# Keeping late loads and state work behind the MLP tiles in a fused memory attention and MLP kernel

## The chip, the cores and the metric

The kernel runs on one core of a Trainium2 chip. The metric is the device time of one execution in microseconds, lower is better. Besides plain times there is one profiled execution, which the hardware profiler recorded instruction by instruction. The engines in that profile are PE (TensorE matmul, with PEld for its weight loads), DVE (VectorE), ACT (ScalarE), POOL (GpSimd) and SP (SyncE, which here only issues DMA transfers). SPq and ACTq are the DMA issues of SP and ACT.

## The reference

Eight batches hold eight heads of 512 tokens with 64 numbers each (x), and each head has a state of 32 vectors. Tokens read from the state and the state reads from the tokens. Both results of a batch, 544 rows of 512 numbers, go through an MLP with a squared ReLU.

```python
scores  = scale * x @ state.T           # softmax over the 32 vectors -> a
xread   = a @ state
scores2 = scale * state @ x.T           # softmax over the 512 tokens -> a2
sread   = a2 @ x
rows    = concat([xread, sread], axis=2) -> (8 * 544, 512)
out     = relu(rows @ w_in) ** 2 @ w_out      # w_in 512 x 2048, w_out 2048 x 512
```

w_in and w_out come as doubles. They are read as pairs of 32-bit words and turned into singles on the chip.

## The kernel before, in words

For the token rows the kernel never forms xread. Since xread = a @ state for each head, xread @ w_in = a @ z with z = state @ w_in, where z has 256 rows for a batch (eight heads of 32 vectors), in two groups of 128. z is made once for each half of the batches: batches 0 to 3 early (`z_part` with G = 0), batches 4 to 7 later. It is written to DRAM tiles (`zd`) and fetched for each batch and each 256 columns (`z_fetch`, tile `z_raw`).

**Precision.** Most operands are split in two (`split`, lines 96 to 98): ACT casts a high part, another engine subtracts it to get the low part. A product is then three matmuls. The first two batches' scores and the first six pieces of z are computed in plain fp32 instead (`PLAIN_X`, `PLAIN_Z`).

**The MLP tile.** The main loop goes through 144 MLP tiles. A tile takes 128 of the 2048 hidden columns for 512 rows: `up` makes six matmuls (L392, tile `ph`), then ReLU on ACT (L394), the square on ACT for the first ten tiles and on DVE (L398) after them, and a split into `g_hi` and `g_lo`. `down`, two tiles later, makes twelve matmuls (L418) into the four sums `po0` to `po3`. Counting tiles from 0, the order is batch 0 (tiles 0 to 5), batch 1 (6 to 15), batch 0 again (16 to 25), batch 1 again (26 to 31), batch 2 from tile 32, batch 3 from tile 48 and so on to tile 127. The last 16 tiles are the 256 state rows. When a batch's part ends, DVE and ACT copy or add the four `po` into the batch's result (L437, L439; L599 where a first part is there already).

**What surrounds the tiles.** Each column block of w_in is loaded (L156, `w_raw`, 512 KB), turned into singles (`singles`: L108 on ACT, then L109, L113, L117 on DVE, tile `wf`), written back to DRAM for later (L162), and multiplied with the state into z (L191 plain, L203 split). Each row block of w_out is loaded (`wo_load`, L444), converted by the same lines (tile `wof`) and split (`wo_hi`, `wo_lo`). For each batch, `pad` loads and splits the state (`sp_raw`, `sp_hl`), `load_t` and `load_n` load x in two layouts (`xt_raw`, `xn_raw`, 512 KB each, two groups a batch), `cut_t` and `cut_n` split them, `scores` makes the scores (`pst`, or `pq` and `st`), `soft1` and `soft1b` make the softmax for the tokens, ending with a transpose into `at` (L327) and the split into `a_hi`, `a_lo`. `turn` scales the exponentials of the second softmax (L338 to L340) and transposes them on PE, `read` makes sread.

**What sets the order.** The program text calls these steps between the MLP tiles: `Ahead` spreads them evenly up to a due tile (two slots a tile). That order is not binding. A scheduler that builds the program with its own timing model may issue an instruction earlier on its engine's queue, if its inputs and buffers are there. Every engine, and SP's DMA issues, then run their queue strictly in order. An instruction that waits holds up all behind it on its engine. `tc.issue_after(i)` adds a constraint for the scheduler: what is traced inside the block and runs on the engine of i is queued behind i. It is a rule of order, with no wait at run time.

Raw loads of weights share four buffers (tag `raw`), x loads two (`xraw`). The scores' PSUM tiles and those of z share two banks (`px`), and `ph` has two.

Of the kernel before, what the change touches and what calls it, by code (L numbers as in the profile page):

```python
# [9 lines left out]
F32 = mybir.dt.float32  # L10
# [8 lines left out]
def memory_attention_then_relu2_ffn(  # L19
# [22 lines left out]
    nc = tc.nc  # L42
# [3 lines left out]
    H = C // D  # L46
# [47 lines left out]
            zd[G, k] = dr.tile([P, NG, HG, FW], F32, name=f"zd_{G}_{k}")  # L94

    def split(hi, lo, src, eng_lo):
        nc.scalar.copy(out=hi, in_=src)  # L97
        eng_lo.tensor_sub(out=lo, in0=src, in1=hi.bitcast(F32))  # L98

    def singles(out_f, words):  # L100

        low, high = words[..., 0], words[..., 1]
        bits = out_f.bitcast(I32)
        nc.scalar.activation(out_f, high.bitcast(F32), AF.Abs, scale=2.0**-112)  # L108
        nc.vector.tensor_scalar(  # L109
            out=bits, in0=bits, scalar1=3, scalar2=0x7FFFFFF8,  # L110
            op0=ALU.logical_shift_left, op1=ALU.bitwise_and,
        )
        nc.vector.scalar_tensor_tensor(  # L113
            out=bits, in0=high, scalar=-0x80000000, in1=bits,
            op0=ALU.bitwise_and, op1=ALU.bitwise_or,
        )
        nc.vector.scalar_tensor_tensor(  # L117
            out=bits, in0=low, scalar=29, in1=bits,
            op0=ALU.logical_shift_right, op1=ALU.bitwise_or,
        )  # L120


    def z_state(G):
        if G == 0:
            raw = sb.tile([P, H, GB * N], F32, name="st_f", tag="x_hl", bufs=1)
            st["raw"] = raw
        else:
            raw = sb.tile([P, H, GB * N], F32, name="st_raw", tag="raw", bufs=RAW)
        for j in range(2):
            nc.sync.dma_start(out=raw[j * D:(j + 1) * D].rearrange("d h m -> d (h m)"), in_=stT[G])  # L130
        hi = sb.tile([P, H, GB * N], F32R, name="stz_hi", bufs=1)
        lo = sb.tile([P, H, GB * N], F32R, name="stz_lo", bufs=1)
        if G:
            split(hi, lo, raw, nc.gpsimd)
        else:
            for i in range(2):
                own = slice(i * D, (i + 1) * D)
                other = slice((1 - i) * D, (2 - i) * D)
                for v in (hi, lo):
                    nc.gpsimd.memset(v[other, i::2, :].bitcast(F32), 0.0)  # L140
                split(hi[own, i::2, :], lo[own, i::2, :], raw[own, i::2, :], nc.vector)
        st[G] = hi, lo

    def z_part(G, k, g):
# [5 lines left out]
        def load():  # L150
            if G:
                box["wf"] = sb.tile([P, nq, FW], F32, name="wf", bufs=2)
                nc.sync.dma_start(out=box["wf"], in_=wd[k][:, ccs, :])
                return
            raw = sb.tile([P, nq, FW, 2], I32, name="w_raw", tag="raw", bufs=RAW)
            nc.sync.dma_start(out=raw.rearrange("p c f w -> p (c f w)"), in_=w_in[k * NG + g])  # L156
            box["raw"] = raw

        def convert():
            wf = sb.tile([P, nq, FW], F32, name="wf", bufs=2)  # L160
            singles(wf, box["raw"])
            nc.sync.dma_start(out=wd[k][:, ccs, :], in_=wf)  # L162
            box["wf"] = wf

# [216 lines left out]
    def mlp(width, fcs, first, rows, aux):  # L381

        nt = width // P
        po = []
        gs = {}
        last = len(fcs) - 1

        def up(fc):
            ph = ps_h.tile([P, S], F32, name="ph", tag="ph")[:, :width]
            todo = first(fc)  # L390
            for i, (w, v) in enumerate(todo):
                nc.tensor.matmul(ph, lhsT=w, rhs=v, start=i == 0, stop=i == len(todo) - 1)  # L392
            r = sb.tile([P, S], F32, name="r", bufs=2)[:, :width]
            nc.scalar.activation(r, ph, AF.Relu)  # L394
            if units[0] < 10:
                nc.scalar.activation(ph, r, AF.Square)
            else:
                nc.vector.tensor_mul(out=ph, in0=ph, in1=r)  # L398
            units[0] += 1
            hi = sb.tile([P, S], F32R, name="g_hi", bufs=2)[:, :width]  # L400
            lo = sb.tile([P, S], F32R, name="g_lo", bufs=2)[:, :width]
            split(hi, lo, ph, nc.vector)
            gs[fc] = hi, lo

        def down(i):
            fc = fcs[i]
            hi, lo = gs.pop(fc)
            if not po:
                po.extend(
                    ps_o.tile([P, DM], F32, name=f"po{t}", tag="po") for t in range(nt)  # L410
                )
            todo = [(t, j) for t in range(nt) for j in range(3)]
            if i < last:
                todo.sort(key=lambda tj: tj[1] == 2)
            for t, j in todo:
                g = (hi, hi, lo)[j][:, t * P:(t + 1) * P]
                w = wo[fc // FPC][j % 2][:, fc % FPC, :]
                nc.tensor.matmul(  # L418
                    po[t], lhsT=g, rhs=w, start=i == 0 and j == 0, stop=i == last and j == 2
                )  # L420
# [257 lines left out]
```

## Time and profile before

| what | value |
|---|---|
| time, median of 3 runs | 707.23 us (707.12 to 707.27) |
| profiled execution, its own time | 708.43 us |
| span of the profiled execution | 706.6 us |
| PE busy | 669.8 us (95%) |
| DVE, ACT, POOL busy | 452.2, 398.3, 199.3 us |
| bytes moved by DMA | 90.58 MB |
| mean clock granted to TensorE | 0.973 |

The profile gives start and duration of each instruction, what its engine waited for, and the granted TensorE clock. Matmuls are pipelined: one of 512 columns is shown as some 400 ns long, while the next one starts much sooner. The reading has to go by stage, since the first hundred microseconds and the rest have different limits. The time of the profiled execution is 1.8 us above its span, and 1.2 us above the median of the plain runs.

### The profile page before, as it was taken

The numbers are of one execution on the slowest core, as the hardware profiler recorded it, in microseconds if no ns is written. First come the engines' busy times: TensorE is split into PE (matmuls) and PEld (weight loads), VectorE is DVE, ScalarE is ACT, GpSimd is POOL, SyncE is SP. The second block draws the span as 40 slices with busy tenths as digits, with TensorE's granted clock in tenths as the row PEclk, the third lists the DMA queues.
The fourth block names the chain that finished last, engine by engine and source line by source line (L and its number), as shares of the span: only waits on it lengthen the run. The fifth ranks groups of instructions, "written<-read, shape, count | busy, mean of one in ns | idle before, by whom it ended". The sixth has DMA issues, their size and how long they took to land.

```text
span 706.6 us, 9753 instructions
## 1 busy us (share of the span) xinstructions
PE 669.8 (95%) x3152; PEld 551.6 (78%) x3152; DVE 452.2 (64%) x757; ACT 398.3 (56%) x727; POOL 199.3 (28%) x181
## 2 busy tenths in 40 slices
PE   4688789999999999999999999999999999999997
PEld 2355668778888888888888878888888888888996
DVE  4859999758456944447945794797944445443553
ACT  3767687567565863467735653665654344332442
POOL 2314433345443540053403240344242022000000
PEclk8589999999999999999999999999999999999999
DMA  8898899435363542344423312412241112100421
GB/s 276 270 315 283 258 306 315 131 97 153 98 202 122 166 149 62 102 135 120 135 78 120 87 48 74 139 58 90 89 150 61 30 31 90 31 16 0 130 80 32
DMA packets 74548, 90.58 MB, mean 128 GB/s; under 512 B 7680, under 2 KB 57600, under 8 KB 74496
## 3 DMA queue, kind: packets, MB, share of 16 engines
q1 hardware_dynamic: 56896, 72.90, 32.9%
q10 hardware_dynamic: 17600, 17.04, 7.1%
q8 instruction: 25, 0.41, 0.3%
q14 instruction: 27, 0.22, 0.1%
HBM read 60.03 MB, written 29.88 MB: 127 GB/s over the span
## 4 chain that ended last, share of the span: by engine, by line
PE 79%; DVE 8%; DMA 6%; issue 2%; ACT 2%; SPq 1%; POOL 0%; DVEq 0%; ACTq 0%; POOLq 0%
PE po L418 47%; PE ph L392 25%; PE pz L203 3%; DMA wo_raw<-w_out 2%; PE pr L355 2%; DMA sp_raw<-stP 2%; PE pq L288 1%; PE pt L343 1%; DVE wf L117 1%; DVE wf L113 1%; DVE z_lo L98 1%; DVE g_lo L98 1%; DMA zd<-z_stage 1%; DMA xt_raw<-xT 1%; DVE wf L109 1%
## 5 line engine op out<-in xcount | busy, mean ns | idle before, releaser
L418 PE MATMUL po<-wo_hi,g_hi 128*128 128x512 f32 x544 | 217.3, 400 | 0.6 <-ACT g_hi L97 0.5
L418 PE MATMUL po<-wo_lo,g_hi 128*128 128x512 f32 x544 | 215.0, 395 | 0.0
L398 DVE TENSOR_TENSOR ph<-ph,r 128x512 f32<-128x512 f32 (+1 forms) x134 | 89.1, 665 | 169.1 <-ACT r L394 168.9
L394 ACT ACTIVATE r<-ph 128x512 f32<-128x512 f32 (+1 forms) x144 | 82.1, 572 | 171.0 <-PE ph L392 169.6
L418 PE MATMUL po<-wo_hi,g_lo 128*128 128x512 f32 x544 | 152.2, 392 | 0.0
L418 PEld LDWEIGHTS po<-wo_hi,g_hi 128*128 128x128 f32 x544 | 103.9, 191 | 22.4 <-ACT g_hi L97 2.0
L418 PEld LDWEIGHTS po<-wo_lo,g_hi 128*128 128x128 f32 x544 | 103.9, 191 | 19.5
L418 PEld LDWEIGHTS po<-wo_hi,g_lo 128*128 128x128 f32 x544 | 101.5, 189 | 21.1 <-issue 1.0
L98 DVE TENSOR_TENSOR g_lo<-ph,g_hi 128x512 fp32r<-128x512 f32 (+1 forms) x144 | 94.4, 656 | 36.3 <-ACT g_hi L97 27.7
L97 ACT CAST g_hi<-ph 128x512 fp32r<-128x512 f32 (+1 forms) x144 | 81.0, 563 | 57.9 <-DVE ph L398 51.7
L392 PE MATMUL ph<-a_hi,z_hi 128*128 128x512 f32 x256 | 81.4, 399 | 2.6 <-DVE nm L306 1.5
L392 PE MATMUL ph<-a_lo,z_hi 128*128 128x512 f32 x256 | 80.1, 392 | 0.0
L392 PE MATMUL ph<-a_hi,z_lo 128*128 128x512 f32 x256 | 80.0, 394 | 0.0
L98 POOL TENSOR_TENSOR xn_hl<-xn_raw,xn_hl 128x1024 fp32r<-128x1024 f32 x16 | 38.9, 2432 | 138.0 <-ACT xn_hl L97 71.2
L182 POOL TENSOR_TENSOR w<-wf,w 64x512 fp32r<-64x512 f32 x32 | 43.0, 1343 | 74.9 <-ACT w L181 69.8
L392 PEld LDWEIGHTS ph<-a_hi,z_hi 128*128 128x128 f32 x256 | 47.6, 190 | 15.2 <-DVE g_lo L98 2.1
L392 PEld LDWEIGHTS ph<-a_hi,z_lo 128*128 128x128 f32 x256 | 48.5, 190 | 10.4
L392 PEld LDWEIGHTS ph<-a_lo,z_hi 128*128 128x128 f32 x256 | 48.2, 189 | 10.5 <-issue 0.3
L98 POOL TENSOR_TENSOR xt_hl<-xt_raw,xt_hl 128x1024 fp32r<-128x1024 f32 x12 | 28.9, 2406 | 75.4 <-ACT xt_hl L97 43.7
L98 DVE TENSOR_TENSOR z_lo<-z_raw,z_hi 128x512 fp32r<-128x512 f32 x64 | 47.9, 750 | 0.3 <-DMA wd<-wf 0.3
L97 ACT CAST z_hi<-z_raw 128x512 fp32r<-128x512 f32 x64 | 39.2, 615 | 1.3 <-DMA wd<-wf 0.8
L98 POOL TENSOR_TENSOR wo_lo<-wof,wo_hi 128x512 fp32r<-128x512 f32 x16 | 25.2, 1578 | 51.4 <-ACT wo_hi L97 51.4
(97 smaller groups left out, 833.7 us busy)
## 6 DMA issues: line engine op xcount, KB each, us to landing
zd<-z_stage ACTq DMA_DIRECT2D x64, 256.0 KB, 3.2
z_raw<-zd SPq DMA_DIRECT2D x252, 64.0 KB, 2.4
xt_raw<-xT SPq DMA_DIRECT2D x16, 512.0 KB, 3.8
w_raw<-w_in SPq DMA_DIRECT2D x16, 512.0 KB, 5.3
wo_raw<-w_out SPq DMA_DIRECT2D x16, 512.0 KB, 5.8
xn_raw<-xn SPq DMA_DIRECT2D x16, 512.0 KB, 3.9
out<-sum SPq DMA_DIRECT2D x32, 256.0 KB, 2.5
wd<-wf SPq DMA_DIRECT2D x16, 256.0 KB, 3.7
```

Of the source, the lines that this page charges most:

```text
L97: nc.scalar.copy(out=hi, in_=src)
L98: eng_lo.tensor_sub(out=lo, in0=src, in1=hi.bitcast(F32))
L109: nc.vector.tensor_scalar(out=bits, in0=bits, scalar1=3, scalar2=0x7FFFFFF8, op0=ALU.logical_shift_left, op1=ALU.bitwise_and,)
L113: nc.vector.scalar_tensor_tensor(out=bits, in0=high, scalar=-0x80000000, in1=bits, op0=ALU.bitwise_and, op1=ALU.bitwise_or,)
L117: nc.vector.scalar_tensor_tensor(out=bits, in0=low, scalar=29, in1=bits, op0=ALU.logical_shift_right, op1=ALU.bitwise_or,)
L182: nc.gpsimd.tensor_sub(out=w[other], in0=wf[own], in1=w[own].bitcast(F32))
L203: nc.tensor.matmul(pz[:, q, :], lhsT=a[:, h, :], rhs=w, start=j == 0, stop=j == len(todo) - 1,)
L355: nc.tensor.matmul(pr[:, q].rearrange("p i c -> p (i c)"), lhsT=my["e"][:, t, q].rearrange("p i n -> p (i n)"), rhs=my["xn"][:, t, q].rear ...
L392: nc.tensor.matmul(ph, lhsT=w, rhs=v, start=i == 0, stop=i == len(todo) - 1)
L394: nc.scalar.activation(r, ph, AF.Relu)
L398: nc.vector.tensor_mul(out=ph, in0=ph, in1=r)
L418: nc.tensor.matmul(po[t], lhsT=g, rhs=w, start=i == 0 and j == 0, stop=i == last and j == 2)
```

## The change

The change does three things.

1. It keeps some steps back. `marks` remembers, for each engine, the latest weight load on SP (L156, L444) and the latest split of an MLP tile on ACT and DVE, as traced so far. The steps in `late` are traced behind these marks: `pad` of batches 2 to 7, every `turn`, and `load_t` and `load_n` of batches 1 to 7. Their instructions on SP, ACT and DVE then cannot be queued ahead of the mark.
2. The state for z of the first four batches (`st_f`) is loaded with only the heads that each half of the rows uses: 4 of 8 heads, 128 KB instead of 256 KB for each half, in pieces of 512 bytes instead of 4096.
3. The split of that state (`z_state_cut`) is traced after the conversions of the first four w_in blocks and the first z products, and on DVE behind the last conversion step of the second block.

No arithmetic is added or removed.

```diff
+    def behind_marks():
+        stack = ExitStack()
+        for i in marks.values():
+            stack.enter_context(tc.issue_after(i))
+        return stack
...
         for j in range(2):
-            nc.sync.dma_start(out=raw[j * D:(j + 1) * D].rearrange("d h m -> d (h m)"), in_=stT[G])
+
+            heads = slice(None) if G else slice(j, None, 2)
+            nc.sync.dma_start(out=raw[j * D:(j + 1) * D, heads, :], in_=stT[G, :, heads, :])
...
-            nc.sync.dma_start(out=raw.rearrange("p c f w -> p (c f w)"), in_=w_in[k * NG + g])
+            mark(nc.sync.dma_start(out=raw.rearrange("p c f w -> p (c f w)"), in_=w_in[k * NG + g]))
...
-            split(hi, lo, ph, nc.vector)
+            mark(*split(hi, lo, ph, nc.vector))
...
-        nc.sync.dma_start(
+        mark(nc.sync.dma_start(
             out=raw.rearrange("p e w -> p (e w)"), in_=w_out[fc * P:(fc + 1) * P, :]
-        )
+        ))
...
     def emit(step):
-        step()
+        with behind_marks() if step in late else ExitStack():
+            step()
...
+    late = {attentions[b][1] for b in range(PLAIN_X, B)}
+    late |= {w["turn"] for b in range(B) for w in attentions[b][2]}
+    late |= {w[n] for b in range(1, B) for w in attentions[b][2] for n in ("load_t", "load_n")}
...
-        q["cut_t"], q["scores"], q["soft1"], p["soft1b"], q["soft1b"], lambda: z_state(0),
+        q["cut_t"], q["scores"], q["soft1"], p["soft1b"], q["soft1b"], lambda: z_state_load(0),
         z0[0][1], z0[0][2], z0[1][1], z0[1][2], *z0[0][3], *z0[1][3], z0[2][0], z0[3][0],
     ):
         emit(s_)
+
+    with tc.issue_after(z0[1][4]["done"].ins):
+        z_state_cut(0)
```

Adding lines moves line numbers: L162 before is L186 after, L156 is L180, L444 is L468, L245 is L269, L264 is L288, L340 is L364, L599 is L631, L327 is L351, L392 is L416, L418 is L442.

Three places of the built order matter later. The first is the queue of SP at the start of the program. Before:

```order
L130 DMA st_f<-stT 64x1024 x2
L156 DMA w_raw<-w_in 128x1024 x2
L245 DMA sp_raw<-stP 128x128 x2
L264 DMA xt_raw<-xT 128x2x512 x2
L162 DMA wd_83<-wf 128x512
L156 DMA w_raw<-w_in 128x1024
L245 DMA sp_raw<-stP 128x128 x2
L162 DMA wd_83<-wf 128x512
L444 DMA wo_raw<-w_out 128x1024
```

With the change:

```order
L150 DMA st_f<-stT 64x4x128 x2
L180 DMA w_raw<-w_in 128x1024 x2
L269 DMA sp_raw<-stP 128x128
L186 DMA wd_83<-wf 128x512
L180 DMA w_raw<-w_in 128x1024
L186 DMA wd_83<-wf 128x512
L468 DMA wo_raw<-w_out 128x1024
```

The states of batches 2 to 4 and both x loads of batch 1 have left this place. The x loads of batch 1 now stand behind the third and the fifth w_out load, those of batch 2 behind the last w_out load.

The second place is the start of DVE's queue, where the second w_in block is converted (`wf_188` before, `wf_178` now). Before:

```order
L338 TENSOR_SCALAR s2_130<-s2_130 128x1
L322 TENSOR_REDUCE s1_151<-q1_124 128x16
L315 TENSOR_REDUCE m1_147<-q1_139 128x16
L306 TENSOR_SCALAR nm2_141<-nm2_141 128x1
L98 TENSOR_TENSOR sp_hl_77<-sp_raw_1688,sp_hl_77 64x4x32 x2
L117 SCALAR_TENSOR_TENSOR wf_188<-w_raw_119,wf_188 128x512
L339 RECIPROCAL s2_130<-s2_130 128x1
L323 TENSOR_SCALAR s1_151<-s1_151 128x16
L338 TENSOR_SCALAR s2_145<-s2_145 128x1
L340 TENSOR_SCALAR e2_129<-e2_129,s2_130 128x512
```

With the change:

```order
L339 TENSOR_REDUCE m1_147<-q1_139 128x16
L346 TENSOR_REDUCE s1_151<-q1_124 128x16
L330 TENSOR_SCALAR nm2_141<-nm2_141 128x1
L131 SCALAR_TENSOR_TENSOR wf_178<-w_raw_119,wf_178 128x512
L98 TENSOR_TENSOR stz_lo_222<-st_f_169,stz_hi_221 64x4x128 x2
L347 TENSOR_SCALAR s1_151<-s1_151 128x16
L123 TENSOR_SCALAR wf_249<-wf_249 128x512
```

The split of batch 2's state (`sp_hl`) and the scaling of the second softmax of batch 0 (`s2`, `e2`) are gone from here, and the split of the state for z (`stz_lo`) moved behind the conversion. The scaling of batch 1, too, no longer stands among the first tiles.

The third place is DVE's queue where batch 2 begins (tile 32). `at_1896` is the second head group of batch 2's softmax, from which `a_hi` comes; `ph_1877` is tile 31, `ph_1944` tile 32; `sum_1238` is batch 1's result. Before, `at_1896` stood at tile 22:

```order
L338 TENSOR_SCALAR s2_1827<-s2_1827 128x1
L339 RECIPROCAL s2_1827<-s2_1827 128x1
L340 TENSOR_SCALAR e2_1826<-e2_1826,s2_1827 128x512
L98 TENSOR_TENSOR g_lo_1474<-ph_1463,g_hi_1473 128x512
L322 TENSOR_REDUCE s1_1891<-q1_1821 128x16
L398 TENSOR_TENSOR ph_1509<-ph_1509,r_1525 128x512
L323 TENSOR_SCALAR s1_1891<-s1_1891 128x16
L98 TENSOR_TENSOR e_hl_2035<-pt_2030,e_hl_2035 128x8x64
L324 RECIPROCAL s1_1891<-s1_1891 128x16
L98 TENSOR_TENSOR g_lo_1529<-ph_1509,g_hi_1528 128x512
L327 STREAM_TRANSPOSE at_1896<-q1_1821 128x512
```

With the change it stands at the end of tile 31:

```order
L98 TENSOR_TENSOR g_lo_1888<-ph_1877,g_hi_1887 128x512
L346 TENSOR_REDUCE s1_1891<-q1_1821 128x16
L347 TENSOR_SCALAR s1_1891<-s1_1891 128x16
L348 RECIPROCAL s1_1891<-s1_1891 128x16
L631 TENSOR_TENSOR sum_1238<-sum_1238,po0_1759 128x512
L631 TENSOR_TENSOR sum_1238<-sum_1238,po1_1760 128x512
L631 TENSOR_TENSOR sum_1238<-sum_1238,po2_1761 128x512
L631 TENSOR_TENSOR sum_1238<-sum_1238,po3_1762 128x512
L351 STREAM_TRANSPOSE at_1896<-q1_1821 128x512
L422 TENSOR_TENSOR ph_1944<-ph_1944,r_1960 128x512
```

The four adds that need the finished sums of tile 31 now stand ahead of the transpose that tile 32 needs. On PE, the place is this, with the change:

```order
L442 MATMUL po3_1762<-wo_hi7_1383,g_lo_1888 128x512
L416 MATMUL ph_1989<-a_hi_1686,z_hi_1950 128x512
L416 MATMUL ph_1944<-a_hi_1686,z_hi_1950 128x512
L416 MATMUL ph_1944<-a_hi_1686,z_lo_1951 128x512 x2
L416 MATMUL ph_1944<-a_lo_1687,z_hi_1950 128x512
```

The first row is the last product of tile 31, and `ph_1989` is tile 33. The third row is the first that reads the second head group of `a_hi`.

More of the change, by code (lines that the diff above doesn't have):

```diff
@@ L96, in split, with mark @@
     def split(hi, lo, src, eng_lo):
-        nc.scalar.copy(out=hi, in_=src)
-        eng_lo.tensor_sub(out=lo, in0=src, in1=hi.bitcast(F32))
+        a = nc.scalar.copy(out=hi, in_=src)
+        return a, eng_lo.tensor_sub(out=lo, in0=src, in1=hi.bitcast(F32))
+    marks = {}
+    def mark(*those):
+        for i in those:
+            marks[i.ins.engine] = i.ins
+    def behind_marks():
[3 more added lines that the diff above has]
+        return stack
     def singles(out_f, words):
@@ L116, in singles @@
         )
-        nc.vector.scalar_tensor_tensor(
+        return nc.vector.scalar_tensor_tensor(
             out=bits, in0=low, scalar=29, in1=bits,
@@ L123, in z_state, with z_state_load @@
     def z_state(G):
+        z_state_load(G)
+        z_state_cut(G)
+    def z_state_load(G):
         if G == 0:
@@ L129, in z_state, with z_state_cut @@
         for j in range(2):
-            nc.sync.dma_start(out=raw[j * D:(j + 1) * D].rearrange("d h m -> d (h m)"), in_=stT[G])
+            heads = slice(None) if G else slice(j, None, 2)
+            nc.sync.dma_start(out=raw[j * D:(j + 1) * D, heads, :], in_=stT[G, :, heads, :])
+        st["raw", G] = raw
+    def z_state_cut(G):
+        raw = st["raw", G]
         hi = sb.tile([P, H, GB * N], F32R, name="stz_hi", bufs=1)
@@ L160, in convert @@
             wf = sb.tile([P, nq, FW], F32, name="wf", bufs=2)
-            singles(wf, box["raw"])
+            box["done"] = singles(wf, box["raw"])
             nc.sync.dma_start(out=wd[k][:, ccs, :], in_=wf)
@@ L218, in product @@
             return run
-        return load, convert, cut, [product(i) for i in range(2)]
+        return load, convert, cut, [product(i) for i in range(2)], box
     def z_fetch(b, k):
@@ L503, in memory_attention_then_relu2_ffn @@
     zs = [[z_part(G, k, g) for k in range(NFCH) for g in range(NG)] for G in range(NGB)]
+    late = {attentions[b][1] for b in range(PLAIN_X, B)}
+    late |= {w["turn"] for b in range(B) for w in attentions[b][2]}
+    late |= {w[n] for b in range(1, B) for w in attentions[b][2] for n in ("load_t", "load_n")}
     lags = {}
-    for _, _, c, ps in zs[0] + zs[1]:
+    for _, _, c, ps, _ in zs[0] + zs[1]:
         lags[ps[0]] = [(c, 2)]
@@ L657 @@
             state.reshape(B * N // 128, 128 // N, H, N, D).transpose(0, 4, 2, 1, 3)
-        ).reshape(B * N // 128, D, H * 128),
+        ),
         "stP": np.ascontiguousarray(
```

## The prediction, made before the result was known

> **What bounds the kernel now.** I read the page first, then the busy time by stage, then PE's waits.
>
> ```profile
> span 706.6 us, 9753 instructions
> PE   4688789999999999999999999999999999999997
> DVE  4859999758456944447945794797944445443553
> ```
>
> PE is full from the seventh of the 40 slices on. Only the start has room. By stage (columns: stretch, its length, busy us of PE, PEld, DVE, ACT and POOL with instruction counts, granted TensorE clock, DMA share, GB/s):
>
> ```profile
> 0.00:28.50 28.50, 12.34 (x32) 6.06 (x32) 16.45 (x36) 15.68 (x34) 9.44 (x17) 0.73 0.86 276
> 28.50:43.00 14.50, 11.09 (x33) 6.85 (x33) 11.41 (x19) 10.44 (x21) 4.75 (x4) 0.74 0.89 293
> 43.00:53.00 10.00, 10.00 (x30) 6.96 (x31) 5.55 (x11) 4.44 (x9) 1.28 (x1) 0.78 0.88 311
> 53.00:70.00 17.00, 14.55 (x59) 10.59 (x58) 15.32 (x27) 13.25 (x25) 7.68 (x5) 0.90 0.84 279
> 70.00:100.00 30.00, 22.40 (x110) 18.46 (x111) 29.93 (x49) 22.47 (x44) 11.17 (x7) 0.92 0.88 283
> 100.00:130.00 30.00, 30.00 (x143) 25.30 (x142) 29.42 (x43) 20.88 (x38) 10.71 (x7) 0.97 0.88 281
> 130.00:160.00 30.00, 28.68 (x132) 23.47 (x131) 17.64 (x29) 20.42 (x36) 12.26 (x8) 1.00 0.34 99
> 160.00:240.00 80.00, 79.72 (x387) 66.88 (x386) 55.13 (x96) 51.63 (x95) 36.68 (x30) 1.00 0.48 149
> 240.00:655.00 415.00, 414.50 (x1947) 345.44 (x1946) 247.26 (x407) 218.18 (x384) 105.28 (x103) 1.00 0.27 83
> ```
>
> PE is idle 16.2 us before 28.5, 3.4 in the next stretch, 2.5 in 53 to 70 and 7.6 in 70 to 100: 29.6 us. From 100 to 655 it is idle 2.1 us. From 70 to 130 DVE is full (29.93 and 29.42 of 30) and DMA busy at 0.88. So the start is bound by weights that arrive and are converted, its second part by DVE; after it every microsecond that PE waits is lost. PE's waits (us in total, times, longest):
>
> ```profile
> PE pz L191 <- DVE wf L117: 11.7, 4, 4.0
> PE pst L298 <- DMA xt_raw<-xT: 4.9, 1, 4.9
> PE pz L203 <- ACT w L97: 2.5, 2, 2.2
> PE ph L392 <- DVE nm L306: 1.5, 1, 1.5
> ```
>
> The largest is for converted w_in blocks; the fourth is the one long stall after 100 us, in the stretch 130 to 160.
>
> **The change at the start.** By the built order these DVE instructions leave the part ahead of tile 6: the split of batch 2's state and the four scalings of the second softmax of batches 0 and 1, with eight one-column steps. Their rows, and two others that matter (start, us, what):
>
> ```profile
> 18.79 1.33 DVE L98 TENSOR_TENSOR sp_hl<-sp_raw,sp_hl 64x128 fp32r<-64x128 f32 x2
> 21.43 0.48 DVE L340 TENSOR_SCALAR e<-e,s 128x512 f32<-128x512 f32 x1
> 22.34 1.27 DVE L340 TENSOR_SCALAR e<-e,s 128x512 f32<-128x512 f32 x1
> 60.96 0.14 DVE L338 TENSOR_SCALAR s<-s 128x1 f32<-128x1 f32 x1
> 62.87 0.47 DVE L340 TENSOR_SCALAR e<-e,s 128x512 f32<-128x512 f32 x1
> 65.32 2.47 DVE L98 TENSOR_TENSOR w<-wf,w 128x512 fp32r<-128x512 f32 x1 [1.61 <-ACT w L97]
> 77.34 0.41 DVE L109 TENSOR_SCALAR wof<-wof 128x512 int32<-128x512 int32 x1
> 78.86 0.68 DVE L117 SCALAR_TENSOR_TENSOR wof<-wo_raw,wof 128x512 int32<-128x512 int32 x1
> 80.13 0.68 DVE L98 TENSOR_TENSOR w<-wf,w 128x512 fp32r<-128x512 f32 x1
> 81.41 1.51 DVE L340 TENSOR_SCALAR e<-e,s 128x512 f32<-128x512 f32 x1
> ```
>
> The split is 1.33, the scalings 0.48 + 1.27 + 0.47 + 1.51 = 3.73, the small steps 8 times 0.15 = 1.2: 6.3 us. One split of a weight took 2.47 instead of 0.68 while POOL split batch 2's x; that work leaves too, so 1.8 more. Against that, the order pulls one w_out conversion (0.41 + 0.68 + 0.68) and one weight split (0.68) ahead of tile 6: 2.45. Net 6.3 + 1.8 - 2.45 = 5.6 us of DVE work less.
>
> What of this is gain? Where DVE is full, 70 to 100, and PE idle, a DVE microsecond is a PE microsecond. Before 70 DVE itself is idle 12.05 + 3.09 + 4.45 + 1.68 = 21 us, waiting for w_in, so work removed there may only lengthen that idle time. Lower bound of the gain 0: all falls there. Upper bound: all PE idle time of 53 to 100 disappears, 2.45 + 7.60 = 10. I take 4.5, nearer to 5.6 than to either end, since the stretched split and the 1.51 scaling (3.3 us net) lie where DVE is the bound. A gain of 0 to 0.9 us from the shorter state load (256 KB less at 276 GB/s), ahead of which PE waits 4.9 us for x, is inside this.
>
> The transfers taken from the start, by the order three x loads of 512 KB (two of batch 2, one of batch 0's second layout), three states of 64 KB and 256 KB of z's state, are 1984 KB, or 7.2 us at 283 GB/s. They free the queue for w_in and w_out, which shortens the same waits; I do not add it to the DVE gain. The x loads of batch 1, moved behind the third and fifth w_out load, are read only after tile 5; with a landing some 6 us from issue I cost them at nothing. If they came late, tile 6 would wait.
>
> The waits of 130 to 160 (1.32) and 160 to 655 (0.78) are shuffled by the new order: between 0 and -2.1, taken -1.0.
>
> **The change at tile 32.** Batch 2's softmax, done by tile 22 before, now comes at tiles 29 to 31, and the order puts four `sum` adds of tile 31 ahead of the transpose into `at`. The rows (first the chain of waits: start, us on PE; then DVE's timeline; then groups: busy us, mean ns | idle before them):
>
> ```profile
> 185.46 4.53 PE po L418 x20
> 163.57 1.40 DVE L294 TENSOR_TENSOR st<-pq,st_low 64x512 f32<-64x512 f32 x2 [0.36 <-ACT st_low L293]
> 176.88 0.71 DVE L327 STREAM_TRANSPOSE at<-q 128x512 f32<-128x512 f32 x1 [1.29 <-POOL q L325]
> L599 DVE TENSOR_TENSOR sum<-sum,po 128x512 f32<-128x512 f32 x8 | 5.2, 679 | 0.0
> L327 DVE STREAM_TRANSPOSE at<-q 128x512 f32<-128x512 f32 x16 | 11.3, 706 | 2.8 <-POOL q L325 2.5
> L97 ACT CAST a_hi<-at 128x512 fp32r<-128x512 f32 x16 | 9.8, 620 | 10.4 <-DVE at L327 8.4 <-PE ph L392 1.9
> L394 ACT ACTIVATE r<-ph 128x512 f32<-128x512 f32 x128 | 75.9, 595 | 145.4 <-PE ph L392 144.0 <-DMA z_raw<-zd 0.6 <-ACT z_stage L215 0.4
> L398 DVE TENSOR_TENSOR ph<-ph,r 128x512 f32<-128x512 f32 x118 | 82.2, 696 | 146.9 <-ACT r L394 146.6
> L97 ACT CAST g_hi<-ph 128x512 fp32r<-128x512 f32 x128 | 75.0, 587 | 56.9 <-DVE ph L398 50.7 <-PE po L418 2.7 <-PE ph L392 2.3
> ```
>
> A product takes 4.53 / 20 = 0.2265 us. The first add waits for `po0`, finished four products before the last, so at T0 (PE's last product of tile 31) less some 0.7 the adds begin. Four times 0.679 brings them to T0 + 2.0, `at` to 2.7, `a_hi` to 3.35. PE has one product behind T0, 0.23: it waits **3.1**. Without the adds, the softmax chain itself, 163.57 to 177.59 = 14.0 us in the old place, stands against some 47 products and 8 half ones, 11.6 us, that PE has from the scores to T0: a wait of the same size, so dropping the adds' share would not save it all. Lower bound 0: the adds or the softmax run ahead of this estimate, as far as `po` allows.
>
> Then the ten products left of tiles 32 and 33 run 2.3 us, to T0 + 5.6. Tile 32's `down` needs r 0.595, square 0.696, g_hi 0.587, one z cast in between on ACT at 0.6; 2.5 us less what overlaps the second tile's products. `ph` has two buffers, so no later `up` can start. PE waits again, **2.3**. What follows is slow matmuls: the next rows show a wait of 2.18 and one of 1.08 and PE after it.
>
> ```profile
> 97.50 0.39 PE L203 MATMUL pz<-w,stz_lo 128*128 128x256 f32 x1 [2.18 <-ACT w L97]
> 99.09 0.58 PE L203 MATMUL pz<-w,stz_hi 128*128 128x256 f32 x1 [1.08 <-DVE w L98]
> 101.39 0.63 PE L418 MATMUL po<-wo_hi,g_hi 128*128 128x512 f32 x1
> 101.81 0.47 PE L418 MATMUL po<-wo_lo,g_hi 128*128 128x512 f32 x1
> ```
>
> Starts 0.42 apart instead of 0.23, from 99.1 to 101.8: half rate, 2.7 us in which 1.35 are lost. I take 1.5 for tile 32, bounds 0 and 2.5. [...]
>
> Sum at tile 32: 3.1 + 2.3 + 1.5 = 6.9; I take 6.5, since the first wait of 3.1 assumes that every piece runs at its mean. Bounds 2.5 (the refill of the pipeline alone, if `a_hi` is in time but tile 32's `up` not ahead) and 9 (a softmax 2 us later).
>
> **Sum.** -4.5 - 1.0 + 6.5 = +1.0. The profiled execution's own time is 708.43, so 709.4 in its terms. It lies 1.2 above the median of 707.23, so the forecast is **708.2 us**.
>
> **Rivals.** B, the start gives everything. 70 to 100 is full of DVE work and the transfers free 7.2 us as well; if all 10 us of PE's idle time there go and tile 32 costs 5: 707.23 - 10 + 5 = 702.2. For it: DVE's 29.93 of 30. Against: PE waits longest for w_in blocks (11.7 us), all of it before 43 us, where DVE has room.
>
> C, slower: the start gives nothing. The pacing chain there is load, cast, three DVE steps and product of each w_in block, whose loads are in the order as before; the removed 6.3 us lay in DVE's idle 21 us and the pulled-ahead conversion eats the rest. Tile 32 stays at 6.5 and the old stalls give 0.5: 707.23 + 6.5 - 0.5 = 713. It decides when the start gains under 4 us, and is clear at 0. For it: DVE idle before 70. Against: 3.3 us of relief after 65 us, where DVE is full.
>
> D, the stall at tile 32 stays small (2.5 or less), since the scheduler put the adds first but the sums of `po` come earlier than I place them: 707.23 - 4.5 - 1 + 2.5 = 704.2. Against: `po3` cannot be finished before T0, and its add stands ahead of `at`.
>
> E, as the forecast, but PE's clock stays full at tile 32: 708.2 - 1.5 = 706.7, no change. For it: the stall of 1.5 in 130 to 160 left the granted clock at 1.00. Against: the rows of 97 to 102 us.
>
> That the change does not do what it says is excluded by the rows of the order.
>
> **How the numbers follow.** Forecast .35, E .15, B .24, C .20, D .06. A measurement of this kernel tells about 0.2% from no change, 1.4 us, so 705.8 to 708.6 is no change. The forecast and E together spread over 705 to 711.5, by the 0 to 10 of the start's gain around its middle; of their .50 I put .10 faster, .21 the same, .19 slower. B (.24) and D (.06, less .01) are faster, C (.20) slower. That is .39, .22 and .39. The range takes in B's 702.2 with a microsecond below it and ends at C's 713: 701 to 713.
>
> **What would show it.** Start: DVE in the stretch 70 to 100 no longer full, PE's waits for `w` and `wf` shorter by 3 to 6 us, the first twelve tiles earlier by as much. B: no idle time of PE between 53 and 100. C: tile 6 at the same time as before. Tile 32: a wait of PE in `ph`, named after `a_hi`, of 2.5 to 3.5 us, with four L631 rows on DVE just ahead of the L351 row; a second of some 2 us in `po` named after `g_hi`; then matmuls 0.42 us apart for 2 to 3 us, and the granted clock of that stretch under 1. E: spacing of 0.23 right after. D: no wait there over 1.5 us. The forecast falls as a whole if any other batch's first tile (48, 64, 80, 96, 112, 128) shows a wait over 1 us, which I have costed at nothing, since their softmax stands tiles ahead in the new order, or if the x of batch 1 comes too late for tile 6.

## The result, and the profile of the changed kernel

The change made the kernel slower: median 716.2 us (715.58 to 717.36) beside 707.25 us before, a ratio of 1.0126 with a 95% interval of 1.0108 to 1.0143. The same kernel on another chip later gave 713.2 beside 707.16, ratio 1.0088 (1.0062 to 1.0115). So it costs 6 to 9 us. The forecast was 708.2 in a range of 701 to 713; both results lie above it.

The changed kernel's profiled execution took 716.28 us, 7.85 more than the one before. Its page, and its busy time by stage from 70 us on (columns as in the prediction; the first 130 us follow further down as one row):

```profile
span 714.1 us, 9749 instructions
...
PE 672.7 (94%) x3152; PEld 554.3 (78%) x3152; DVE 457.6 (64%) x757; ACT 399.0 (56%) x727; POOL 199.5 (28%) x181
```

```profile
70.00:100.00 30.00, 21.94 (x111) 19.13 (x110) 29.97 (x45) 22.34 (x43) 11.67 (x7) 0.89 0.89 283
...
130.00:160.00 30.00, 30.00 (x137) 24.92 (x136) 14.27 (x21) 16.58 (x29) 8.02 (x5) 1.00 0.36 112
160.00:240.00 80.00, 75.01 (x328) 61.10 (x327) 45.35 (x80) 37.89 (x71) 18.32 (x13) 0.96 0.26 84
```

and from there to 655 us:

```profile
240.00:655.00 415.00, 412.87 (x1959) 345.58 (x1958) 263.08 (x440) 234.55 (x412) 129.02 (x123) 1.00 0.30 95
```

From these rows and those of before, PE's idle time by stage:

| stage, us | PE idle before | PE idle after | what the prediction said of it |
|---|---|---|---|
| 0 to 130 | 29.6 | 29.2 | start, -4.5 |
| 130 to 160 | 1.3 | 0.0 | old stalls, -1.0 with the next ones |
| 160 to 240 | 0.3 | 5.0 | tile 32, +6.5 with the slow clock |
| 240 to 655 | 0.5 | 2.1 | nothing |

Idle time explains 4.6 us of the span's 7.5 (over the whole span, 36.8 before and 41.4 after). The rest is PE's longer busy time (672.7 against 669.8). In the stretch 160 to 240 the granted clock was 0.96 instead of 1.00: it stood at 0.50 for two steps of 3.41 us, from 216.32 and from 223.15 on (their rows are in the last section). PE worked through both and lost half of each, 3.4 us. Counted in the same way, by the trace's clock, PE lost 13.8 us up to 130 us before and 14.7 after, so the start did not gain there either.

The new loss stands where the prediction put it, at tile 32. PE's waits there, then DVE's queue:

```profile
215.88 0.50 PE L416 MATMUL ph<-a_hi,z_hi 128*128 128x512 f32 x1 [2.94 <-ACT a_hi L97]
...
221.89 0.50 PE L442 MATMUL po<-wo_hi,g_hi 128*128 128x512 f32 x1 [1.88 <-ACT g_hi L97]
...
223.58 0.63 PE L442 MATMUL po<-wo_hi,g_hi 128*128 128x512 f32 x1
224.01 0.63 PE L442 MATMUL po<-wo_lo,g_hi 128*128 128x512 f32 x1
...
303.90 0.50 PE L442 MATMUL po<-wo_hi,g_hi 128*128 128x512 f32 x1 [1.20 <-ACT g_hi L97]
```

```profile
212.07 2.48 DVE L631 TENSOR_TENSOR sum<-sum,po 128x512 f32<-128x512 f32 x4 [0.56 <-PE po L442]
214.47 0.70 DVE L351 STREAM_TRANSPOSE at<-q 128x512 f32<-128x512 f32 x1
```

The four adds run first, from 212.07, then the transpose; PE goes on 0.7 us after the transpose ends, once `a_hi` is cast, and has waited 2.94 us. The refill of the pipeline costs 1.88. At 223.58 products start 0.43 us apart; the undisturbed spacing was 0.2265. The last PE row, at tile 48, is a wait that the prediction had costed at nothing.

### The profile page after: what moved, and what is told of

Read it like the earlier page. It is cut to its first block, busy times and chain, and to the rows that moved or that the text cites. A ratio compares the mean times of both kernels' runs of the same rounds, so it can differ in the third digit from the quotient of the medians.

```text
span 714.1 us, 9749 instructions
## 1 busy us (share of the span) xinstructions
PE 672.7 (94%) x3152; PEld 554.3 (78%) x3152; DVE 457.6 (64%) x757; ACT 399.0 (56%) x727; POOL 199.5 (28%) x181
## 4 chain that ended last, share of the span: by engine, by line
PE 80%; DMA 7%; DVE 6%; ACT 3%; issue 2%; SPq 1%; ACTq 0%; DVEq 0%
PE po L442 47%; PE ph L416 25%; PE pr L379 2%; PE pz L227 2%; DMA zd<-z_stage 2%; DMA w_raw<-w_in 2%; PE pq L312 2%; DMA wo_raw<-w_out 1%; DVE wof L127 1%; PE pt L367 1%; DMA sp_raw<-stP 1%; DVE wf L127 1%; DVE wf L131 1%; SPq L254 1%; DMA z_raw<-zd 1%
## 5 line engine op out<-in xcount | busy, mean ns | idle before, releaser
L442 PE MATMUL po<-wo_hi,g_hi 128*128 128x512 f32 x544 | 215.8, 397 | 5.2 <-ACT g_hi L97 5.1
L442 PE MATMUL po<-wo_lo,g_hi 128*128 128x512 f32 x544 | 214.4, 394 | 0.0
L418 ACT ACTIVATE r<-ph 128x512 f32<-128x512 f32 (+1 forms) x144 | 82.5, 574 | 158.4 <-PE ph L416 156.1
L442 PE MATMUL po<-wo_hi,g_lo 128*128 128x512 f32 x544 | 152.3, 391 | 0.2 <-DVE g_lo L98 0.2
L442 PEld LDWEIGHTS po<-wo_hi,g_hi 128*128 128x128 f32 x544 | 103.5, 190 | 28.7 <-ACT g_hi L97 7.2
L98 DVE TENSOR_TENSOR g_lo<-ph,g_hi 128x512 fp32r<-128x512 f32 (+1 forms) x144 | 94.4, 656 | 42.1 <-ACT g_hi L97 30.1
L442 PEld LDWEIGHTS po<-wo_lo,g_hi 128*128 128x128 f32 x544 | 103.4, 190 | 20.7 <-issue 0.2
L442 PEld LDWEIGHTS po<-wo_hi,g_lo 128*128 128x128 f32 x544 | 100.8, 188 | 20.4 <-DVE g_lo L98 0.4
L416 PE MATMUL ph<-a_hi,z_hi 128*128 128x512 f32 x256 | 82.0, 400 | 5.3 <-ACT a_hi L97 4.4
L416 PE MATMUL ph<-a_lo,z_hi 128*128 128x512 f32 x256 | 81.7, 396 | 0.0
L416 PE MATMUL ph<-a_hi,z_lo 128*128 128x512 f32 x256 | 81.5, 399 | 0.0
L98 POOL TENSOR_TENSOR xn_hl<-xn_raw,xn_hl 128x1024 fp32r<-128x1024 f32 x16 | 38.5, 2408 | 150.3 <-ACT xn_hl L97 127.0
L416 PEld LDWEIGHTS ph<-a_hi,z_hi 128*128 128x128 f32 x256 | 48.0, 192 | 16.5 <-ACT a_hi L97 5.5
L416 PEld LDWEIGHTS ph<-a_lo,z_hi 128*128 128x128 f32 x256 | 49.1, 192 | 11.2 <-issue 0.7
L416 PEld LDWEIGHTS ph<-a_hi,z_lo 128*128 128x128 f32 x256 | 49.0, 192 | 10.3
L98 POOL TENSOR_TENSOR xt_hl<-xt_raw,xt_hl 128x1024 fp32r<-128x1024 f32 x12 | 28.9, 2405 | 94.4 <-ACT xt_hl L97 71.4
L98 DVE TENSOR_TENSOR z_lo<-z_raw,z_hi 128x512 fp32r<-128x512 f32 x64 | 49.2, 768 | 0.1
L239 ACT COPY z_stage<-pz 128x512 f32<-128x512 f32 x64 | 37.5, 590 | 10.3 <-PE pz L227 5.7
```

Source lines behind the costliest of these rows:

```text
L98: return a, eng_lo.tensor_sub(out=lo, in0=src, in1=hi.bitcast(F32))
L239: nc.scalar.copy(out=stage, in_=pz)
L442: nc.tensor.matmul(po[t], lhsT=g, rhs=w, start=i == 0 and j == 0, stop=i == last and j == 2)
```

## The experiments

Each run's time stands beside runs of the kernel before on the same chip.

| run | median us | ratio to before, 95% interval |
|---|---|---|
| late_only | 718.5 | 1.0151 (1.0129 to 1.0174) |
| state_only | 707.07 | 0.9986 (0.9972 to 1.0000) |
| b2_free | 704.08 | 0.9957 (0.9939 to 0.9976) |
| no_wo_lo | 710.68 | 1.0051 (1.0029 to 1.0074) |
| turn_only | 707.57 | 0.9994 (0.9978 to 1.0011) |
| adds_behind | 710.58 | 1.0040 (1.0021 to 1.0058) |
| fill_gaps | 709.68 | 1.0013 (0.9989 to 1.0037) |
| b2_free_lo_dve | 704.52 | 0.9958 (0.9943 to 0.9972) |
| change_again | 713.21 | 1.0088 (1.0062 to 1.0115) |
| b2_free_again | 704.51 | 0.9944 (0.9923 to 0.9966) |
| b1_b2_free | 704.87 | 0.9963 (0.9950 to 0.9976) |

### Which part loses: late steps or the state for z

late_only, the state as before:

```diff
-            heads = slice(None) if G else slice(j, None, 2)
+            heads = slice(None)
...
-        ... q["soft1b"], lambda: z_state_load(0),
+        ... q["soft1b"], lambda: z_state(0),
...
-    with tc.issue_after(z0[1][4]["done"].ins):
-        z_state_cut(0)
```

> The late steps as in the change; the state for z loaded and split as before. Theory (the loss is batch 2's softmax, put behind the marks, at tile 32; the state's part is worth about nothing): 714 to 717.5, with PE waits of about 2.9 and 1.9 us at tile 32 and two half-rate pieces, as in the changed kernel. Rival (the state load in 512-byte pieces and the moved split cost the start what the late loads gave it): 711 to 713.

state_only, the state as in the change:

```diff
-    late = {attentions[b][1] for b in range(PLAIN_X, B)}
-    late |= ...
+    late = set()
```

> The state for z loaded by halves and split later, as in the change; no step is late. Theory: 705.5 to 708, no wait over 1.6 us behind 100 us. Rival (the state's part costs): 709 to 711, with PE's first matmul at 6.4 us instead of 4.9 and no gain before 100 us.

turn_only, only the second softmaxes late:

```diff
-    late = {attentions[b][1] for b in range(PLAIN_X, B)}
+    late = {w["turn"] for b in range(B) for w in attentions[b][2]}
-    late |= ...
```

> Only the steps that scale and transpose the second softmax are late; loads, states and the state for z as before. If DVE work at the start is what counts: the four scalings and eight small steps (4.9 us) leave it, and at the rate of the run without w_out's low parts (5.5 us won for 13 us of DVE time) that is 2 us: 704 to 706.5. If they fell into DVE's idle time: 706.5 to 708.

The state's part alone gains at most 0.3% and late turns alone change nothing that can be told. late_only is 1.5% slower (718.5 where 714 to 717.5 were expected) and no faster than the change. So the loss comes in with the late loads and states, and the state's part, if anything, takes a little of it back. The rival that the 512-byte pieces of the state's load cost the start is out: in state_only PE's first matmul came when it did before, after a wait of 4.9 us. (With the same pieces the changed kernel waited 6.5 us there in its first profile and 5.0 in its second.)

```profile
4.89 5.27 PE L322 MATMUL pst<-xt_raw,sp_f 128*128 128x512 f32 x8 [4.89 <-DMA xt_raw<-xT]
```

### Batch 2 set free

```diff
-    late = {attentions[b][1] for b in range(PLAIN_X, B)}
+    late = {attentions[b][1] for b in range(PLAIN_X + 1, B)}
...
-    late |= {w[n] for b in range(1, B) ... for n in ("load_t", "load_n")}
+    late |= {w[n] for b in range(1, B) ... for n in ("load_t", "load_n") if (b, n) != (2, "load_t")}
```

> The change without lateness for batch 2's state and its x loads for the scores; all other late steps stay. Theory: the two waits (4.8 us) and the half rate (3 us) at tile 32 go, 716.2 - 7.7 = 708.5, between 706 and 710. Rival (the late second softmaxes, or the later batches, carry the loss): 712 to 716, with waits of PE at other places.

> Batch 2 not late, again. If its gain over the kernel before is real: ratio 0.994 to 0.998. Against the changed kernel on the same chip the sum of what the trace showed (7.7 at tile 32, 1.2 at tile 48, 1 in 100 to 130) makes it 10 us faster.

Taking batch 2's state and its two x loads out of the late steps turns a loss into a gain, twice: 0.9957 and 0.9944. The first time came out below the 706 to 710 that were expected. On one chip it was 8.7 us faster than the change (704.51 against 713.21), where 10 were expected. Rows of b2_free from 130 to 240 us:

```profile
130.00:160.00 30.00, 30.00 (x141) 25.07 (x140) 18.34 (x31) 20.77 (x37) 13.76 (x9) 1.00 0.38 119
160.00:240.00 80.00, 80.00 (x376) 67.01 (x375) 46.75 (x76) 38.45 (x70) 17.90 (x15) 1.00 0.29 94
```

PE has no idle time from 130 to 240 and the clock is full. This is the version to keep: some 3 us faster than the kernel before. Its profiles show 1.3 us of this in the old stalls of 130 to 160. In the start PE is idle 27.7 and 28.4 us, against 29.6; but profiles of the change, adds_behind and fill_gaps, which have the same order up to tile 31, lie between 26.0 and 31.1 there, so that part is not shown.

### What makes tile 32 late

adds_behind queues the four adds behind the transpose:

```diff
+            turned[b] = nc.vector.transpose(out=at, in_=q1.rearrange("p j n -> p (j n)"))
...
-                nc.vector.tensor_add(out=sums[b][:, t, :], in0=sums[b][:, t, :], in1=po)
+                with tc.issue_after(turned[2].ins) if b == 1 else ExitStack():
+                    nc.vector.tensor_add(out=sums[b][:, t, :], in0=sums[b][:, t, :], in1=po)
```

> The change, with the four sum adds of tile 31 queued behind the transpose into at that tile 32 needs. If the adds are what makes tile 32 late, the first wait falls from 2.9 to about 1.2 us (the softmax chain itself, whose multiplication on POOL ends about 0.2 us after PE's last product of tile 31, then 0.7 and 0.6) and with less half rate the time to 713 to 715. If the softmax is late anyway by as much, the wait stays near 2.9 and the time at 716.

PE's two waits in that run, and the stretch around them:

```profile
212.36 0.50 PE L416 MATMUL ph<-a_hi,z_hi 128*128 128x512 f32 x1 [1.23 <-ACT a_hi L97]
...
216.86 0.50 PE L442 MATMUL po<-wo_hi,g_hi 128*128 128x512 f32 x1 [1.94 <-ACT g_hi L97]
```

```profile
160.00:240.00 80.00, 76.65 (x353) 63.09 (x352) 50.64 (x85) 41.59 (x76) 22.28 (x18) 1.00 0.28 90
```

The first wait fell to 1.23, as expected from the softmax chain alone. The adds are 1.7 us of the 2.94, and the clock stayed full. The time fell to 1.0040; against the change's 1.0088 and 1.0126 that is 3.4 to 6.1 us where 1 to 3 were expected. The half clock (1.5 us in one profile of the change, 3.4 in the other) and the wait of 1.2 at tile 48, which is gone here too, make up the rest.

fill_gaps puts useless products into the gaps (`lastmm` holds the MLP matmul traced last):

```diff
+    def fill(n):
+        dm = ps_x.tile([P, S], F32, name="dm", tag="px")
+        with tc.issue_after(lastmm["pe"].ins):
+            for _ in range(n):
+                nc.tensor.matmul(dm, lhsT=wo[0][0][:, 0, :P], rhs=wo[0][0][:, 0, :], start=True, stop=True)
...
+                if units[0] == 34 and i == 1:
+                    fill(4)
...
+        if b == 2:
+            fill(11)
         mlp(S, fcs, first, rows, aux)
```

> The change with useless products in the two gaps of tile 32: 11 (2.5 us) behind tile 31 and 4 (0.9 us, with the z products that move there) behind tile 33's first half. They add work and shorten no wait. If the gaps cost 3 us more by the half rate behind them, spacing stays at 0.23 us and the time falls to 712.5 to 714.5. If the clock is not ruled by these gaps: 716 to 717.

```profile
160.00:240.00 80.00, 79.86 (x370) 66.54 (x369) 49.56 (x85) 41.11 (x75) 20.96 (x17) 1.00 0.27 88
```

With 15 x 0.2265 = 3.4 us of useless work the clock stays at 1.00 in this stretch, and the kernel is no slower than before within its interval. Added work that shortens a run shows that the gap's price is more than the gap. Against the change's 1.0088 and 1.0126 the gain is 5 to 8 us where 2 to 4 were expected. The first profile accounts for 6.1: 4.9 us less idle time in this stretch (other products moved into the gaps too) and no half clock, 3.4, less the useless 3.4, and the wait at tile 48, 1.2, which went here too.

### Why the start gave nothing

no_wo_lo leaves out the low part of w_out, and with it 16 subtractions on POOL. The product with the low part reads the high part a second time, so the matmuls are as many and the output is not the reference's:

```diff
-        split(wo[k][0][:, i, :], wo[k][1][:, i, :], wf, nc.gpsimd)
+        nc.scalar.copy(out=wo[k][0][:, i, :], in_=wf)
...
-                w = wo[fc // FPC][j % 2][:, fc % FPC, :]
+                w = wo[fc // FPC][0][:, fc % FPC, :]
```

> The change, but the low part of w_out is not made: POOL's 16 subtractions (23 us in the first 130) are left out and the product with the low part reads the high part once more. The matmuls are as many. DVE instructions that ran beside a POOL subtraction were 1 us longer than alone, 8.7 us in all. Theory (the start is bound by DVE, whose steps POOL lengthens; what the change took off DVE came back as that lengthening): 5 to 8 us faster than the change, 708 to 711. Rival (the start is bound by the arrival of weights): 715 to 716.5.

The first 130 us of the kernel before, of the changed kernel, of this run and of b2_free, one row each:

```profile
0.00:130.00 130.00, 100.38 (x403) 74.22 (x403) 108.09 (x179) 87.15 (x165) 45.02 (x40) 0.86 0.87 284
```

```profile
0.00:130.00 130.00, 100.79 (x409) 74.90 (x410) 108.99 (x167) 87.97 (x167) 44.16 (x41) 0.86 0.87 280
```

```profile
0.00:130.00 130.00, 103.56 (x438) 77.99 (x439) 98.78 (x171) 92.16 (x175) 24.81 (x28) 0.88 0.91 293
```

```profile
0.00:130.00 130.00, 102.30 (x417) 75.80 (x418) 112.78 (x170) 89.24 (x169) 44.05 (x40) 0.87 0.85 283
```

The change has 12 DVE instructions fewer in this stretch (167 against 179), and DVE is busy 0.9 us longer. The six kinds of conversion step, 16 of each in both, took 76.0 us instead of 70.9; two kinds got slower, four a little faster. The second step of w_out (L113 before, L127 now) went from a mean of 0.84 us to 1.05.

In the trace, every DVE instruction of these 130 us that took over 0.25 us longer than the shortest of its kind ran beside a POOL operation: 19 before, 25 after, 11 in no_wo_lo. Without w_out's subtractions on POOL the DVE time falls by 10.2 us (108.99 to 98.78), with the same conversions. The run is at 1.0051, against 1.0088 and 1.0126 of the change, so 10.2 us of DVE time are worth 2.6 to 5.3 us, about half at most. That they are worth anything is not clear of noise: the interval overlaps that of the change's second run, and POOL was relieved by 19 us as well. And b2_free, faster than both, has DVE busy longest of the four (112.78). DVE's busy time alone does not set the start.

PE's waits in these 130 us show where the relief went (us in total, times, longest). Beside the prediction's rows, the kernel before has these:

```profile
PE pz L203 <- DVE w L98: 2.0, 2, 1.1
PE pz L191 <- ACT z_stage L215: 2.7, 1, 2.7
PE pz L203 <- ACT z_stage L215: 1.5, 1, 1.5
```

The changed kernel:

```profile
PE pz L227 <- ACT z_stage L239: 8.4, 4, 3.5
...
PE pz L215 <- DVE wf L131: 4.2, 2, 2.2
PE pz L215 <- ACT a_hi L97: 3.0, 1, 3.0
PE pz L215 <- ACT z_stage L239: 1.9, 1, 1.9
...
PE ph L416 <- ACT a_hi L97: 1.4, 1, 1.4
```

Waits that ended with a converted or split weight (`wf`, `w`) came to 16.2 us before. In the changed kernel they are 4.2, or 7.2 with the 3.0 that the view puts down to `a_hi`: that product does not read `a_hi`, and its w_in block was ready at 23.73, 0.15 us before it began. (The second profile has 6.2, or 9.2.) Waits that ended with ACT's copy of z out of PSUM (`z_stage`) rose from 4.2 to 10.3, and to 10.5 in the second profile. So converted weights held PE up less, and PE then waited for ACT's copies instead. ACT's queue shows one way. The copy that ended the wait of 3.00 us before 77.48 stood behind the cast of a w_out block, for which ACT itself had waited on DVE:

```profile
74.82 0.62 ACT L97 CAST wo_hi<-wof 128x512 fp32r<-128x512 f32 x1 [3.55 <-DVE wof L131]
...
76.83 0.60 ACT L239 COPY z_stage<-pz 128x512 f32<-128x512 f32 x1
```

No run moves these copies, so that they hold the start back now is read from the waits and not tested.

b2_free_lo_dve, with batch 2 free and w_out's subtractions on DVE, asks whether less DVE time in all is then a gain:

```diff
-        split(wo[k][0][:, i, :], wo[k][1][:, i, :], wf, nc.gpsimd)
+        split(wo[k][0][:, i, :], wo[k][1][:, i, :], wf, nc.vector)
```

> Batch 2 free, and the low parts of w_out made by DVE instead of POOL: DVE gets 16 instructions of 0.68 us (10.9 us) and loses the lengthening by POOL that the run without them showed (13 us). If DVE's time in all sets the start: 2 us less DVE time, 703 to 704.5. If the order of DVE's queue counts more (w_in conversions now stand behind these splits): 704.5 to 708.

It equals b2_free (0.9958 against 0.9957), although DVE is busy 4.5 us less up to 130 us (108.26 against 112.78). Its time ends up at the edge of both expectations (704.52) and does not tell them apart. In its profile PE waits 2.4 us for DVE's `g_lo` between 130 and 160, which b2_free does not have.

b1_b2_free lets batch 1's x loads go early again as well (and the second layout of batch 2's):

```diff
-    late |= {w[n] for b in range(1, B) ... if (b, n) != (2, "load_t")}
+    late |= {w[n] for b in range(3, B) for w in attentions[b][2] for n in ("load_t", "load_n")}
```

> Batch 2 and also batch 1's x loads not late. The loads of batch 1 then stand ahead of the third w_in block again, 1 MB or 3.6 us of transfer. If the start is bound by the arrival of weights, it loses 2 to 4 us against the run with batch 2 free: 706 to 708. If DVE's time binds it, they are equal within 1 us: 703 to 705.

1 MB of loads ahead of the third w_in block again cost 0.4 us against b2_free on the same chip (704.87 against 704.51), within the intervals. So the transfers that the change took out of the start were worth nothing that can be told, and a start bound by the arrival of weights alone is not supported.

### How steady the price is

> The changed kernel once more, on one chip with the next two. If the first comparison holds whatever the chip: 1.011 to 1.014 times the time before, some 716. If the start of a run varies from chip to chip by the 2 to 3 us that profiles with the same order up to tile 31 show, the ratio comes out at 1.008 to 1.011.

The second chip gave 1.0088, at the upper end of the second expectation. PE's waits at tile 32 in that profile:

```profile
215.39 0.50 PE L416 MATMUL ph<-a_hi,z_hi 128*128 128x512 f32 x1 [2.94 <-ACT a_hi L97]
...
221.06 0.50 PE L442 MATMUL po<-wo_hi,g_hi 128*128 128x512 f32 x1 [1.74 <-ACT g_hi L97]
```

The waits are the same 2.94 and about the same 1.74. But this execution has only one step at half clock, behind the first wait, and PE worked 3.08 us of it: 1.5 us lost against 3.4. That accounts for 1.9 us of the 2.6 us between the two profiled executions (716.28 and 713.67). Another 0.5 lies in the start, where the add to batch 0's sum began at 184.97 us in one and 185.45 in the other. Where the gaps fell among the steps of the two, the last section shows.

## Why the prediction was wrong, point by point

**What bounds the kernel.** Right for the part behind 130 us: PE's idle time and its loss at half clock grew there by 8.4 us. With 0.5 from the start that is 8.9, and the span grew by 7.5; the other 1.4 are not explained.

**The start, -4.5: this term failed.** PE's idle time up to 130 us went from 29.6 to 29.2. Two steps behind the 4.5 were wrong. First, the DVE time removed was counted by the durations of the rows, 1.27 and 1.51 us for scalings that take 0.47 alone; both ran beside POOL. Summed over the first 130 us with the shortest duration of each kind, DVE's instructions came to 98.5 us before and 96.2 after: 2.3 us less work and not 5.6. What they took beyond it rose from 21.4 to 24.4, with POOL about as busy as before (44.2 against 45.0 us), and so DVE was busy 0.9 us more. That also ate the 1.8 us of the stretched weight split. Second, a DVE microsecond was taken for a PE microsecond where DVE is full and PE idle. The prediction's sign for the gain, waits for `w` and `wf` shorter by 3 to 6 us, came true with 9.0 us (7.0 in the second profile), and PE's idle time hardly moved: waits for ACT's `z_stage` grew by 6.1, and smaller ones, for x, `a_hi` and `g_hi`, by most of the rest. Its other signs failed: DVE was full in 70 to 100 as before (29.97 of 30), and the copies of batch 0's first sum, behind tile 5, began at 92.33 us instead of 91.20.

**Old stalls, -1.0.** The idle time of 130 to 160 went (1.3 us), but tile 48 got a wait of 1.2 and 240 to 655 as a whole 1.6. Net nothing. A wait over 1 us there was the prediction's sign that the forecast falls as a whole. No late softmax made it: `g_hi` of tile 48 was cast at 303.26, behind two casts of weights and a copy of z that ACT ran from 301.50 on, and the wait is gone in adds_behind, fill_gaps and b2_free, which keep batch 3 as late. The prediction also misplaced a row: the wait of 1.5 us for `nm`, which it put into 130 to 160, stands at 71.49. The stretch had two shorter ones, 0.57 and 0.75 us.

```profile
71.49 0.73 PE L392 MATMUL ph<-a_hi,z_hi 128*128 128x512 f32 x2 [1.49 <-DVE nm L306]
```

**Tile 32, +6.5.** The mechanism was right to the row: adds ahead of the transpose, a first wait of 2.94 (3.1 said), a refill of 1.88 (2.3 said), half rate. Half rate was mis-sized: 3.4 us in the first profile and 1.5 in the second, where 1.5 was taken with an upper bound of 2.5. It came behind both waits in the first profile, and the prediction had it behind the second alone. The step from the worked-out 6.9 to 6.5 went the wrong way for the first profile; the sum came to 2.94 + 1.88 + 3.4 = 8.2 and 2.94 + 1.74 + 1.5 = 6.2. The prediction also said that dropping the adds would not save it all: right, 1.23 us stay.

**Rivals.** C, a start that gives nothing with tile 32 at its price, is what happened, at 713 forecast and 713.2 to 716.2 measured, and it had a chance of .20. That its number came so near was in part luck, for its reason does not hold: it had the chain from load to product of each w_in block pace the start, and the waits for that chain are the ones that fell. B and D are out: the start's idle time stayed and both waits came. E, a full clock at tile 32, is out for the changed kernel; in adds_behind, with waits of 1.23 and 1.94 us, it held. Part of E's ground, a stall of 1.5 us in 130 to 160 that left the clock full, was the misplaced row.

**The range** ended at C's 713 with tile 32 at 6.5. C with that term's own upper bound of 9 would have reached 715.5. Two terms had bounds, and the range let only one of them go to its end.

## What to carry to other kernels

A constraint that keeps early work out of a crowded start also removes the slack that this work had: ask for each deferred chain whether it ends before its first reader, and exempt the one whose reader comes first. A DVE instruction that looked long beside POOL was worth only its own length here when it was removed (1.27 and 1.51 us beside POOL, 0.47 alone), and more of the others were long (25 where there had been 19). A wait that shrinks is not yet a gain: look which wait comes next in the same stage, on another engine's queue. And the gaps on PE cost more than themselves here where the clock dropped behind them (2.94 and 1.88 us, and 3.4 us more at half clock), so a first wait shortened by 1.7 us won more than that (3.4 to 6.1 us in adds_behind).

## What the runs showed of the hardware

**DVE beside POOL.** POOL's rows, then DVE's, in the changed kernel:

```profile
52.35 1.28 POOL L98 TENSOR_TENSOR wo_lo<-wof,wo_hi 128x512 fp32r<-128x512 f32 x1 [4.90 <-ACT wo_hi L97]
...
75.52 2.28 POOL L98 TENSOR_TENSOR wo_lo<-wof,wo_hi 128x512 fp32r<-128x512 f32 x1 [3.14 <-ACT wo_hi L97]
77.76 1.50 POOL L349 TENSOR_TENSOR q<-q,s 128x512 f32<-128x512 f32 x1
```

```profile
74.11 0.68 DVE L131 SCALAR_TENSOR_TENSOR wof<-wo_raw,wof 128x512 int32<-128x512 int32 x1
...
75.99 0.68 DVE L127 SCALAR_TENSOR_TENSOR wof<-wo_raw,wof 128x512 int32<-128x512 int32 x1
...
76.75 1.59 DVE L131 SCALAR_TENSOR_TENSOR wf<-w_raw,wf 128x512 int32<-128x512 int32 x1
78.27 1.53 DVE L131 SCALAR_TENSOR_TENSOR wof<-wo_raw,wof 128x512 int32<-128x512 int32 x1
```

With POOL idle an L131 instruction took 0.68 (74.11). The two long ones end at 78.34 and 79.80, each 0.54 us after a POOL operation ends (77.80 and 79.26). All 25 long DVE instructions counted above for the changed kernel end in this way behind a POOL operation: the seven of L123 0.28 to 0.29 us behind its end (they take 0.38 at their shortest), the 18 others, of L127, L131 and L98, 0.55 us (0.63 to 0.66 at their shortest). They last 0.66 to 2.83 us and yet end at these two distances. That looks like a wait for POOL and then a run, rather than a slow run beside it; the trace does not mark the two apart. In one place the POOL row is the long one: beside the DVE row at 75.99, which took its 0.68, the POOL row at 75.52 took 2.28, and the one at 52.35 took 1.28. So each of the two engines had rows lengthened beside the other; by what, no row shows.

**The clock behind short gaps.** In the traces of the kernel before and of the changed kernel the granted clock is recorded from 9.81 and from 11.52 us on, always as 1.00 or 0.50, and up to its last change it holds each time for a whole number of steps of 3.41 us (1 to 177 of them). Here are such steps (columns as in the prediction) in the changed kernel, in its second profile and in adds_behind:

```profile
212.91:216.32 3.41, 0.47 (x3) 0.40 (x3) 2.26 (x4) 0.62 (x1) 0.42 (x1) 1.00 0.82 307
216.32:219.74 3.42, 3.42 (x10) 2.42 (x8) 0.00 (x0) 0.00 (x0) 0.86 (x1) 0.50 0.02 8
219.74:223.15 3.41, 1.53 (x6) 1.05 (x6) 2.76 (x5) 2.57 (x5) 0.00 (x0) 1.00 0.00 0
223.15:226.56 3.41, 3.41 (x9) 2.64 (x8) 1.04 (x4) 0.00 (x0) 0.00 (x0) 0.50 0.26 77
```

```profile
216.24:219.65 3.41, 3.08 (x8) 1.88 (x6) 0.09 (x1) 0.72 (x2) 0.46 (x1) 0.50 0.00 0
219.65:223.07 3.42, 2.01 (x9) 1.66 (x10) 3.35 (x8) 1.84 (x4) 0.00 (x0) 1.00 0.03 11
223.07:226.48 3.41, 3.41 (x17) 2.82 (x16) 1.06 (x2) 1.07 (x2) 0.00 (x0) 1.00 0.25 66
```

```profile
215.31:218.72 3.41, 1.86 (x8) 1.56 (x9) 3.31 (x7) 1.99 (x5) 0.00 (x0) 1.00 0.19 68
218.72:222.13 3.41, 3.41 (x17) 2.83 (x16) 1.19 (x2) 0.94 (x2) 0.00 (x0) 1.00 0.26 73
```

Behind a step at full clock in which PE worked 0.47 or 1.53 us comes one at half clock; behind one with 2.01 or 1.86 us the clock stays full. From 100 to 690 us the traces of the kernel before and of the changed kernel have 344 steps at full clock, and only those two, with 0.47 and 1.53 us of work, are followed by half clock; in the others PE worked 2.21 us or more. Ahead of 100 us PE's busy time does not sort the steps: in the changed kernel one with 1.53 us of work, from 72.95 on, is followed by full clock, and one with 1.69, from 35.42 on, by half clock. In the rows above the 1.88 us of waiting lay within one step; the 1.74 us of the second profile ran across the end of one at 219.65, and the 1.94 of adds_behind across one at 215.31. That goes with the 3.4 us lost in one profile and the 1.5 in the other. These are counts from a few traces, and what sets the clock is not shown.
